# A three-layer kernel: the start of its first feed-forward layer as a written list

## The chip, the cores and the metric

The kernel runs on one NeuronCore of a Trainium2 chip. The engines are TensorE (PE in the rows; its weight loads PEld), VectorE (DVE), ScalarE (ACT), GpSimd (POOL) and SyncE (SP), which here only issues DMAs. Each runs its own queue of instructions in order and waits on semaphores for the others. The metric is the time of one execution on the device in microseconds; a comparison uses the median of several runs.

## The reference

Inputs q, k, v have shape (4, 8, 768, 64): batch, heads, tokens, features. Three layers follow each other:

```
# 1: linear attention with a decay gamma[h] per head
state = gamma * state + outer(k[t], v[t]);  y[t] = q[t] @ state / sqrt(64)      for t in 0..767
x = y as (3072 tokens, 512)
# 2: first feed-forward layer, 512 -> 2048 -> 512
h = x @ w_in;  x = (h * cos(h)) @ w_out
# 3: second feed-forward layer, 512 -> 1536 -> 512
g = x @ w_gate;  out = (silu(g) * (x @ w_val)) @ w_out2
```

## The kernel before

**Tiles.** The 3072 tokens are 24 chunks of 128: six blocks along the sequence for each of four batch rows. Chunks 4j to 4j+3 (one block of all four rows) form token tile j, 512 tokens wide. Chunks 0 to 3 need no state: scores (`scores_pe`), decay (`scores_decay`, three VectorE products for each half), values (`values_pe`). Chunks from 4 on use halves of a chunk: near scores (`near_pe`), a state update (`update_pe`, `update_add`), and values out of the old state and the near scores (`near_values`). GpSimd scales keys (`scale_keys`), queries (`scale_queries`) and the state. The values are split into a high and a low part for the matmuls: ScalarE writes the high one (`split_hi`), VectorE the low one (`split_lo`).

**Units.** The first feed-forward layer works in units. Unit n belongs to a token tile j and a slice m of 128 hidden features. Its hidden product is 12 matmuls of 512 columns (high by high, high by low, low by high, over four slices of features), from `project`. Then come: the turns n (ScalarE), the remainder r (VectorE), Sin and Square (ScalarE), the product with h (VectorE), the high half of g (ScalarE), the low half (VectorE). `output1` multiplies g into four output banks, 12 matmuls, two units later (`SKEW = 2`). Units 0 to 6 are tile 0 with slices 0 to 6 (`HEAD = 7`), unit 7 on is tile 1 from slice 0. After output unit 6 the four banks are evacuated, two by ScalarE and two by VectorE, and stored to DRAM (`x2d`) by four DMAs. Hidden products share two banks (`ps_h`), so the product of unit n waits until unit n-2 has read its own for the last time, in the VectorE product with h.

**Weights.** The 16 slices of weights of this layer come in 64-bit words, 1 MB for each slice, and are converted: abs (ScalarE), clamp (GpSimd), shift of the exponent (`low`, VectorE), `round` (ScalarE), `merge` (VectorE), `hi` (ScalarE), `lo` (VectorE). Weights 0 to 6 are loaded at the start and stay. Weights 7 to 10 and 12 to 15 are loaded later, into the tiles that chunks 7 to 4 and 3 to 0 held before.

**What sets the order.** The kernel writes the order of each engine by hand (`manual_schedule`): what the program calls first stands first on its engine. Before the units a short string lists the work on chunks 0 to 4 and weights 0 and 1. In each unit, `hidden1` places its own steps and those of the weights that `halves_at` gives it (first halves `a`, second halves `b`), and lists of late work (`late_g`, `late_gl`, `late_mid`, `late_x`) are run at fixed places in it. `attn_at` says after which unit the products of chunks 4 to 7 stand. SP issues the loads in the order of the calls. TensorE gets some matmuls with no use (`keep_awake`) in the stretch in which it waits for loads.

Of the kernel before, what the change touches and what calls it, by code (L numbers as in the profile page):

```python
# [46 lines left out]
HEAD = 7  # L47

# [48 lines left out]
def fused(ctx: ExitStack, tc: tile.TileContext, qkv, w1, w2, consts, out):  # L97
# [53 lines left out]
    class Weight:  # L151
# [89 lines left out]
    W1, W2 = [], []  # L241

    def fetch_w1(m):
        assert m == len(W1)
        W1.append(Weight(w1[m], wpool, f"w{m}", w1d.get(m)))
# [39 lines left out]

    qkv_t = {}
# [3 lines left out]
    def load_qk(c, pool=qpool, tag="qkv"):  # L290
        if c >= NCH:
            return
        if pool is wpool:
            both = wpool.tile([P, 4, 512], F32, tag=tag, name="qkv")
            qkv_t[c] = [both[:, 0:2], both[:, 2:4]]
        else:
            qkv_t.setdefault(c, [None, None])[0] = pool.tile([P, 2, 512], F32, tag=tag, name="qk")
        nc.sync.dma_start(out=qkv_t[c][0].rearrange("p a b -> p (a b)"), in_=qkv[c, :, 0:1024])

    def load_kv(c, part=slice(0, 2)):  # L300
        if c >= NCH:
            return
        if qkv_t.setdefault(c, [None, None])[1] is None:
            qkv_t[c][1] = qpool.tile([P, 2, 512], F32, tag="qkv", name="kv")
        n0, n1 = 512 * part.start, 512 * part.stop
        nc.sync.dma_start(
            out=qkv_t[c][1][:, part].rearrange("p a b -> p (a b)"), in_=qkv[c, :, 1024 + n0:1024 + n1]
        )
# [58 lines left out]
    def values_pe(c, places=((ps_a, "a"), (ps_a, "a")), idle=0):  # L367
# [3 lines left out]
        ps_t[c, "rest"] = y2[0][:, 2:4].rearrange("p a (b d) -> p (a b) d", d=D)  # L371
# [51 lines left out]
    def update_add(c, u):  # L423
        st = states[c % B]
        if u == 0:
            nc.vector.tensor_tensor(out=middle, in0=ps_t[c][0][:, 1], in1=st, op=ALU.add)
            return
        old_state[c] = st
        if last_block(c):
            return  # L430
        new = states[c % B] = spares.pop()
        nc.vector.tensor_tensor(out=new, in0=ps_t[c][1][:, 1], in1=middle, op=ALU.add)
        nc.gpsimd.tensor_tensor(
            out=new, in0=new, in1=const(CG, NP).unsqueeze(2).to_broadcast([P, NP, D]), op=ALU.mult
        )
# [5 lines left out]
    def near_values(c, places=((ps_a, "a"), (ps_a, "a"))):  # L441
        qk, kv = qkv_t[c]
        y2 = [p.tile([P, 4, C], F32, tag=t, name="y") for p, t in places]
        y = [t[:, 0:2] for t in y2]
        order = [h for pair in ((0, 2), (1, 3)) for k in pair for h in FEATURES[k]]
# [32 lines left out]
    def state_pe(c, place=(ps_a, "a")):  # L478
        _, kv = qkv_t[c]
        rest = ps_t.pop((c, "rest"))  # L480
        u = place[0].tile([P, NP, D], F32, tag=place[1], name="u") if place else rest
# [10 lines left out]
    def state_add(c):  # L492
        u, st = ps_t.pop((c, "u")), states[c % B]
        nc.vector.tensor_copy(out=st, in_=u)
# [3 lines left out]

    def attn_state(c, place):
        state_pe(c, place)  # L500
        late_mid.append(lambda: state_add(c))
# [6 lines left out]
    def attn_update(c):  # L508
        update_pe(c)
        late_mid.extend(lambda u=u: update_add(c, u) for u in range(2))  # L510
# [52 lines left out]
    def hidden1(j, m, first, a, b, soon):  # L563
        begin(first)
        if not soon:
            each(a, "size")
        h = project(weight1(m, 0), x_t[j], ps_h, "h", "h")
        n = npool.tile([P, T], I32, tag="n", name="n")
        r = tmp.tile([P, T], F32, tag="r", name="r_")
# [5 lines left out]
        nc.scalar.activation(out=n, in_=h, func=AF.Identity, scale=TURN)  # L575
        each(b, "hi")
        if soon:
            each(a, "size")
        each(a, "round")
        run(mid)  # L580
        nc.vector.scalar_tensor_tensor(
            out=r, in0=h, scalar=TURN, in1=n, op0=ALU.mult, op1=ALU.subtract
        )
# [3 lines left out]
        nc.scalar.activation(out=r, in_=r, func=AF.Sin, scale=PI)  # L587
        nc.scalar.activation(out=r, in_=r, func=AF.Square, scale=ROOT2)

        def finish():  # L590
            nc.vector.scalar_tensor_tensor(
                out=r, in0=r, scalar=1.0, in1=h, op0=ALU.subtract, op1=ALU.mult
            )
            g = g_t[1, j, m] = gpool.tile([P, 2, T], F32R, tag="g", name="g")
            nc.scalar.activation(out=g[:, 0], in_=r, func=AF.Copy, scale=-1.0)
            late_gl.append(lambda: nc.vector.scalar_tensor_tensor(
                out=g[:, 1], in0=r, scalar=-1.0, in1=g[:, 0].bitcast(F32), op0=ALU.mult, op1=ALU.subtract
            ))

        late_g.append(finish)  # L600
# [137 lines left out]
    ORDER = ["P1", "P2", "P5", "P6", "P3", "P7", "P4"]  # L738
    next_wo = [0]

    def fetch_wo():
        g, n = divmod(next_wo[0], len(ORDER))
        if g < len(groups2):
# [4 lines left out]
                in_=wod[groups2[g][1]][ORDER.index(order_of(g)[n])],  # L748
# [77 lines left out]
    def order_of(g):  # L826
        return ["P1", "P5", "P2", "P6", "P3", "P7", "P4"] if g == len(groups2) - 1 else ORDER
# [36 lines left out]
    def second_layer():  # L864
# [145 lines left out]
    o2, o3, two = (ps_o, "o2"), (ps_o, "o3"), [(ps_a, "a")] * 2  # L1010

    attn_at = {
        0: [(attn_state, c, place) for c, place in enumerate(two + [o2, o3])]
        + [(attn_update, 4), (scale_queries, 4), (scale_keys, 5)],
        1: [(attn_scores, 5), (attn_values, 4, (o2, o3), False), (attn_update, 5), (scale_keys, 6)],
        2: [(attn_values, 5, two, False)], 3: [(attn_near, 6), (scale_keys, 7)],
        4: [(attn_values, 6, two, False)],
        5: [(attn_near, 7)], 6: [(attn_values, 7, two, False)],
    }
# [43 lines left out]
    with tc.manual_schedule():  # L1063
        warm = tmp.tile([P, T], F32, tag="r", name="warm")
# [9 lines left out]
        queries = slice(CQ, CQ + 512)  # L1074
        head = slice(CG, CQ)
        near = slice(CD, CD + 512)
        keys, values = slice(0, 1), slice(1, 2)
        places = ["w15", "w14", "w13", "w12", "w10", "w9", "w8", "w7"]

        def load_cst(cols):  # L1080
            nc.sync.dma_start(out=const(cols.start, cols.stop - cols.start), in_=consts[:, cols])

        load_qk(0, wpool, places[0])
        for half in range(2):
            nc.sync.dma_start(out=first_dec[half], in_=consts[:, 512 * half:512 * half + 512])
        load_kv(0, values)
        nc.vector.memset(above, ABOVE)
        nc.scalar.activation(out=idle_act, in_=above, func=AF.Sin, scale=2.0**-16)
        load_qk(1, wpool, places[1])
        load_kv(1, values)  # L1090
        fetch_w1(0)
        for c in (2, 3):
            load_qk(c, wpool, places[c])
            load_kv(c, values)
        fetch_w1(1)
        load_cst(head)
        load_kv(0, keys)
        load_qk(CPB, wpool, places[CPB])
        load_cst(near)
        for c in range(1, CPB):  # L1100
            load_kv(c, keys)
        load_cst(queries)
        fetch_w1(2)
        load_kv(CPB)
        load_qk(CPB + 1, wpool, places[CPB + 1])
        load_kv(CPB + 1)
        fetch_w1(3)
        for c in (CPB + 2, CPB + 3):
            fetch_w1(len(W1))
            load_qk(c, wpool, places[c])  # L1110
            load_kv(c)
        fetch_w1(6)

        def first_scores(c):
            if c == CPB:
                near_pe(c, [(ps_o, f"o{half}") for half in range(2)])
                return
            scores_pe(c, [(ps_o, f"o{2 * (c % 2) + half}") for half in range(2)], 4 if c else 0)

        def first_decay(c):  # L1120
            for half in range(2):
                near_decay(c, half) if c == CPB else scores_decay(c, half, c % 2)

        def first_y(c):
            values_pe(c, [(ps_h, "h")] * 2 if c % 2 else [(ps_a, "a")] * 2, 10)

        def first_hi(c):
            first_x[c] = values_x(c)
            for y, x in first_x[c]:
                split_hi(y, x)  # L1130

        def first_lo(c):
            for y, x in first_x[c]:
                split_lo(y, x)

        first_x = {}
        steps = {
            "sc": first_scores, "m": first_decay, "y": first_y, "xh": first_hi,
            "xl": first_lo, "k": scale_keys,
        }  # L1140
        for a in (
            "sc0 m0 y0 sc1 xh0 xl0 m1 size0 y1 xh1 xl1 low0 round0 sc2 m2 y2 merge0 xh2 sc3 m3 hi0 xl2 lo0 size1 "
# [121 lines left out]
```

## Time and profile before

| | us |
|---|---|
| median of 3 runs | 1141.17 |
| lowest and highest | 1140.91, 1143.11 |
| the profiled execution | 1140.55 |
| its span, first to last instruction | 1138.4 |
| TensorE matmuls busy | 1120.1 (98% of the span) |
| VectorE busy | 795.4 (70%) |
| ScalarE busy | 627.0 (55%) |
| GpSimd busy | 120.2 (11%) |

The span is what the rows speak of; about 2 us lie around it. Busy shares are means over the whole execution. The changed part lies in its first 90 us, so windows and timelines of that part are to be read, not the means. Matmuls overlap, so the time of one is best read from the start of one piece to the start of the next.

### The profile page before, as it was taken

The numbers are of one execution on the slowest core, as the hardware profiler recorded it, in microseconds if no ns is written. First come the engines' busy times: TensorE is split into PE (matmuls) and PEld (weight loads), VectorE is DVE, ScalarE is ACT, GpSimd is POOL, SyncE is SP. The second block draws the span as 40 slices with busy tenths as digits, with TensorE's granted clock in tenths as the row PEclk, the third lists the DMA queues.
The fourth block names the chain that finished last, engine by engine and source line by source line (L and its number), as shares of the span: only waits on it lengthen the run. The fifth ranks groups of instructions, "written<-read, shape, count | busy, mean of one in ns | idle before, by whom it ended". The sixth has DMA issues, their size and how long they took to land.

```text
span 1138.4 us, 19049 instructions
## 1 busy us (share of the span) xinstructions
PE 1120.1 (98%) x7704; PEld 914.2 (80%) x7704; DVE 795.4 (70%) x1267; ACT 627.0 (55%) x954; POOL 120.2 (11%) x109
## 2 busy tenths in 40 slices
PE   8899999999999999999999999999999999999998
PEld 5688878888888888888888888887888887888886
DVE  6865774457777677667656566878666879666687
ACT  4868974456667767677755343434343434333431
POOL 3521222111211111110000000000000000000011
PEclk9899999999999999999999999999999999999999
DMA  9616843235997699588774845676656675655534
GB/s 349 244 39 235 318 173 107 86 137 190 330 355 275 246 358 387 192 316 341 277 272 165 318 173 202 256 260 215 237 207 228 230 282 209 230 214 203 185 139 166
DMA packets 62966, 266.00 MB, mean 234 GB/s; under 512 B 6304, under 2 KB 6560, under 8 KB 47264
## 3 DMA queue, kind: packets, MB, share of 16 engines
q1 hardware_dynamic: 62880, 264.80, 63.4%
q8 instruction: 60, 0.98, 0.4%
q14 instruction: 26, 0.21, 0.1%
HBM read 208.68 MB, written 56.10 MB: 233 GB/s over the span
## 4 chain that ended last, share of the span: by engine, by line
PE 83%; ACT 6%; DVE 5%; DMA 4%; issue 1%; SPq 0%; POOL 0%; DVEq 0%; POOLq 0%
PE h L532 20%; PE o L618 20%; PE X L757 15%; PE Z L757 8%; PE oX L843 7%; PE oZ L843 6%; PE Y L757 4%; ACT rw L176 2%; DMA qkv<-in_qkv_dram 2%; DMA kv<-in_qkv_dram 2%; PE y L452 1%; PE y L463 1%; ACT f L160 1%; DMA rw<-in_w_dram 1%; DVE go L804 1%; DVE acc L854 1%
## 5 line engine op out<-in xcount | busy, mean ns | idle before, releaser
L532 PE MATMUL h<-x,w 128*128 128x512 f32 x780 | 191.5, 394 | 2.1 <-DVE x L146 1.4
L618 PE MATMUL o<-g,w 128*128 128x512 f32 x780 | 189.0, 391 | 2.0 <-DVE x L146 2.0
L618 PEld LDWEIGHTS o<-g,w 128*128 128x128 f32 x780 | 147.0, 189 | 33.0 <-issue 2.4
L532 PEld LDWEIGHTS h<-x,w 128*128 128x128 f32 x780 | 144.2, 188 | 34.1 <-DVE x L146 1.6
L757 PE MATMUL X<-xo,wh 128*128 128x512 f32 x576 | 145.4, 389 | 0.0
L757 PEld LDWEIGHTS X<-xo,wh 128*128 128x128 f32 x576 | 108.0, 188 | 22.7 <-DVE xo L718 0.4
L843 PE MATMUL oX<-go,wo 128*128 128x512 f32 x432 | 109.1, 389 | 0.3 <-DVE acc L854 0.3
L804 DVE TENSOR_TENSOR go<-raw,go 128x512 fp32r<-128x512 f32 x126 | 84.6, 709 | 35.0 <-ACT go L802 34.7
L843 PEld LDWEIGHTS oX<-go,wo 128*128 128x128 f32 x432 | 81.0, 188 | 17.5 <-DVE acc L854 0.7
L575 ACT ACTIVATE n<-h 128x512 int32<-128x512 f32 x96 | 57.0, 594 | 66.5 <-PE h L532 65.8
L532 PE MATMUL h<-x,back 128*128 128x512 f32 x372 | 91.0, 393 | 0.0
L176 ACT ACTIVATE rw<-rw,above 128x1024 uint16<-128x1024 uint32 x34 | 89.4, 2629 | 0.0
L618 PE MATMUL o<-g,back 128*128 128x512 f32 x372 | 89.4, 389 | 0.0
L618 PEld LDWEIGHTS o<-g,back 128*128 128x128 f32 x372 | 69.8, 188 | 14.5
L532 PEld LDWEIGHTS h<-x,back 128*128 128x128 f32 x372 | 68.9, 188 | 14.9
L802 ACT ACTIVATE go<-raw 128x512 fp32r<-128x512 f32 x126 | 72.2, 622 | 15.6 <-DVE raw L795 9.9
L843 PE MATMUL oZ<-go,wo 128*128 128x512 f32 x312 | 78.8, 389 | 0.0
L757 PE MATMUL X<-x,wh 128*128 128x512 f32 x288 | 73.4, 390 | 2.8 <-DVE p L980 2.8
L757 PE MATMUL Z<-xo,wh 128*128 128x512 f32 x288 | 73.1, 389 | 0.0
L843 PEld LDWEIGHTS oZ<-go,wo 128*128 128x128 f32 x312 | 58.6, 188 | 12.2
L795 POOL TENSOR_TENSOR raw<-raw 128x512 f32<-128x512 f32 x7 | 10.1, 1450 | 551.2 <-DVE go L804 551.2
L757 PEld LDWEIGHTS X<-x,wh 128*128 128x128 f32 x288 | 53.8, 188 | 15.0 <-issue 2.8
(683 smaller groups left out, 1686.7 us busy)
## 6 DMA issues: line engine op xcount, KB each, us to landing
wh<-w2d SPq DMA_DIRECT2D x36, 1024.0 KB, 6.2
rw<-in_w_dram SPq DMA_DIRECT2D x34, 1024.0 KB, 7.7
wo<-wod SPq DMA_DIRECT2D x63, 512.0 KB, 3.7
back<-w1d SPq DMA_DIRECT2D x31, 1024.0 KB, 7.8
wh<-w2d SPq DMA_DIRECT2D x36, 768.0 KB, 4.8
w2d<-parts SPq DMA_DIRECT2D x12, 1024.0 KB, 4.1
xo<-x2d SPq DMA_DIRECT2D x19, 512.0 KB, 6.7
w1d<-w SPq DMA_DIRECT2D x9, 1024.0 KB, 4.8
```

Source lines behind the costliest of these rows:

```text
L160: nc.scalar.activation(out=self.f, in_=self.raw[:, :, 1].bitcast(F32), func=AF.Abs)
L176: nc.scalar.activation(out=self.raw.bitcast(U16)[:, :, 2], in_=self.raw[:, :, 0].bitcast(U32), func=AF.Identity, scale=2.0**-29, bias=above,)
L452: nc.tensor.matmul(out=y[bank][D * half:D * half + D, slot, HALF * u:HALF * u + HALF], lhsT=st[r, h // 2, :], rhs=qk[r, 0, q0:q0 + HALF], ...
L463: nc.tensor.matmul(out=y[bank][D * half + f:D * half + f + width, slot, HALF * u:HALF * u + HALF], lhsT=kv[r, 1, h * D + f:h * D + f + wid ...
L532: nc.tensor.matmul(out=ps, lhsT=w[:, a, k * P:(k + 1) * P], rhs=x[:, b, k, :], start=n == 0, stop=n == len(order) - 1,)
L575: nc.scalar.activation(out=n, in_=h, func=AF.Identity, scale=TURN)
L618: nc.tensor.matmul(out=o_t[0][i], lhsT=w[:, a, i * P:(i + 1) * P], rhs=g[:, b, :], start=first and n == 0, stop=last and n == 2,)
L757: nc.tensor.matmul(out=ps, lhsT=w[:, a, k * P:(k + 1) * P], rhs=x[:, b, k, :], start=start and n == 0, stop=n == len(order) - 1, skip_grou ...
L802: nc.scalar.activation(out=t[:, i, 0], in_=raw_of(g, i, slot), func=AF.Copy)
L804: nc.vector.tensor_tensor(out=t[:, i, 1], in0=raw_of(g, i, slot), in1=t[:, i, 0].bitcast(F32), op=ALU.subtract)
L843: nc.tensor.matmul(out=ps, lhsT=w[:, i, a, d * P:(d + 1) * P], rhs=x[:, i, b, :], start=start and m == 0, stop=m == len(order) - 1, skip_g ...
L854: nc.vector.tensor_tensor(out=e[:, c], in0=ps[:, c], in1=e[:, c], op=ALU.add)
```

## The change

The string of steps and the calls per unit up to unit 8 are replaced by three tables: `LOADS` (the order of the first loads), `ORDER` (every step on chunks 0 to 7, weights 0 to 6, hidden units 0 to 8 and output units 0 to 6), and `BANKS` (the banks of scores, state products and values). `AWAKE` gives the useless matmuls ahead of three steps: 39, before 52. The list was found by a search over a model of the engines. From unit 9 on the program is as before. `size` becomes `abs` and `clamp`, which the list places apart; keys and values of a chunk are loaded by one function, `load_first`; the state's copy and its decay are two steps; the class `Hidden` holds the steps of a unit. In the list a number is a chunk, a weight or a unit: `h`, `n`, `r`, `sin`, `sq`, `fin`, `ghi`, `glo` are the steps of a hidden unit in the order given above, `o` an output unit, `u` a state product, `U` an update, `y` values, `sc` scores, `da` and `db` the decay of a chunk's halves.

```diff
+SCRIPT = 9
+LOADS = """
+    qk0 dec qk1 w1 v0 qk2 w0 qk3 v1 v3 v2 k2 k0 head k1 w3 qk4 k4 w2 k3 near queries qk5 qk6 v4 k5 w4 v5 k7 v6
+    k6 w5 qk7 w6 v7
+""".split()
+ORDER = """
...
+    ghi5 xb7 sin6 sq6 Xb7 fin6 glo5 h7 h8 o5 n7 ghi6 r7 glo6 o6 n8 r8 sin8 sin7 sq8 sq7 fin7 ghi7 glo7
+""".split()
+AWAKE = {"sc1": 10, "y0": 14, "sc3": 15}
...
+        for name, c in map(split_name, ORDER):
+            if name in steps:
+                steps[name](c)
+            elif hasattr(Hidden, name):
+                getattr(hidden[c], name)()
+            else:
+                getattr(W1[c], name)()
+        late_g.append(hidden[SCRIPT - 1].late)
+        pending.extend(units[SCRIPT - 2:SCRIPT])
+        del w1_halves[:2 * HEAD]
+        fetch_w1(HEAD)
+
-        for n, (kind, j, m, first, last) in enumerate(units):
+        for n, (kind, j, m, first, last) in list(enumerate(units))[SCRIPT:]:
```

What moves, in the order of the instructions. First TensorE around the first hidden unit, before; `u` are state products, `sc` scores or (L409, after L442) updates, `h` hidden units, `w_403`, `w_461` the weights 0 and 1:

```order
L376 MATMUL y<-s,qkv 64x128 x8
L394 MATMUL sc<-qkv 64x64 x16
L532 MATMUL h<-x,w_403 128x512 x12
L484 MATMUL u<-qkv 64x64 x32
L409 MATMUL sc<-qkv 64x64 x16
L532 MATMUL h<-x,w_461 128x512 x12
```

The same place after (there `w_465` is weight 0 and `w_401` weight 1):

```order
L518 MATMUL u<-qkv 64x64 x16
L427 MATMUL sc<-qkv 64x64 x16
L518 MATMUL u<-qkv 64x64 x8
L565 MATMUL h<-x,w_465 128x512 x12
L518 MATMUL u<-qkv 64x64 x8
L565 MATMUL h<-x,w_401 128x512 x12
L442 MATMUL sc<-qkv 64x64 x16
L427 MATMUL sc<-qkv 64x64 x32
```

The state products of chunks 0 to 2 now stand ahead of hidden unit 0, that of chunk 3 between units 0 and 1.

ScalarE around the evacuation of output unit 6 (`ev`), before; `r__1118` belongs to unit 7, `r__1155` to unit 8, `rw_1139` is weight 7:

```order
L587 ACTIVATE r__1118<-r__1118 128x512
L588 ACTIVATE r__1118<-r__1118 128x512
L595 ACTIVATE g<-r__1118 128x512
L575 ACTIVATE n<-h 128x512
L587 ACTIVATE r__1155<-r__1155 128x512
L588 ACTIVATE r__1155<-r__1155 128x512
L545 ACTIVATE ev<-o_707 128x512
L545 ACTIVATE ev<-o_709 128x512
L160 ACTIVATE f<-rw_1139 128x1024
L595 ACTIVATE g<-r__1155 128x512
```

The same place after; `r__1138` belongs to unit 7, `r__1167` to unit 8, `rw_1177` is weight 7:

```order
L578 ACTIVATE ev<-o_841 128x512
L578 ACTIVATE ev<-o_843 128x512
L605 ACTIVATE n<-h 128x512
L614 ACTIVATE r__1167<-r__1167 128x512
L614 ACTIVATE r__1138<-r__1138 128x512
L617 ACTIVATE r__1167<-r__1167 128x512
L617 ACTIVATE r__1138<-r__1138 128x512
L626 ACTIVATE g<-r__1138 128x512
L185 ACTIVATE f<-rw_1177 128x1024
L626 ACTIVATE g<-r__1167 128x512
```

The evacuations now stand ahead of the turns of unit 8 and of the Sin and Square of both units.

SP's loads and stores at that place, before (`x2d` are the stores of the evacuated banks, `rw` loads of weights, `w1d` the write back of a converted weight):

```order
L155 DMA rw_1139<-in_w_dram 128x2048
L628 DMA x2d_90<-ev 128x512 x4
L155 DMA rw_1188<-in_w_dram 128x2048
L155 DMA rw_1234<-in_w_dram 128x2048
L195 DMA w1d_96<-w_1256 128x2048
```

And after:

```order
L687 DMA x2d_90<-ev 128x512 x4
L180 DMA rw_1177<-in_w_dram 128x2048
L180 DMA rw_1179<-in_w_dram 128x2048
L180 DMA rw_1225<-in_w_dram 128x2048
L226 DMA w1d_96<-w_1246 128x2048
```

The load of weight 7 stood ahead of the four stores and now stands behind them.

## Rows read from the trace of the kernel before

**Rows 1.** The page, part 4: the chain of waits, by engine.

```profile
PE 83%; ACT 6%; DVE 5%; DMA 4%; issue 1%; SPq 0%; POOL 0%; DVEq 0%; POOLq 0%
```

**Rows 2.** TensorE's timeline: start, length, line, operation, count, idle before and its releaser.

```profile
5.32 1.22 PE L345 MATMUL sc<-qkv 64*64 64x128 f32 x32 [0.27 <-DMA qkv<-in_qkv_dram]
...
27.60 2.08 PE L484 MATMUL u<-qkv 128*64 128x64 f32 x64
...
47.00 2.90 PE L618 MATMUL o<-g,w 128*128 128x512 f32 x6 [2.04 <-DVE x L146]
...
51.31 3.04 PE L532 MATMUL h<-x,w 128*128 128x512 f32 x12
...
57.00 0.69 PE L394 MATMUL sc<-qkv 64*64 64x64 f32 x32
57.52 0.65 PE L409 MATMUL sc<-qkv 64*64 64x64 f32 x32
58.09 3.02 PE L532 MATMUL h<-x,w 128*128 128x512 f32 x12
...
63.76 0.69 PE L452 MATMUL y<-qkv,st 64*64 64x64 f32 x32
...
65.00 3.02 PE L532 MATMUL h<-x,w 128*128 128x512 f32 x12
...
86.97 2.88 PE L618 MATMUL o<-g,w 128*128 128x512 f32 x12
89.69 2.88 PE L532 MATMUL h<-x,w 128*128 128x512 f32 x12
```

**Rows 3.** Waits of TensorE (90 to 200 us), ScalarE (90 to 160): total, times, longest.

```profile
PE h L532 <- DVE w L146: 0.3, 1, 0.3
PE h L532 <- DVE r__1566 L591: 0.3, 1, 0.3
...
ACT n L575 <- PE h L532: 1.3, 2, 1.0
```

**Rows 4.** ScalarE's timeline.

```profile
34.64 1.21 ACT L160 ACTIVATE f<-rw 128x1024 f32<-128x1024 f32 x1 [0.56 <-DMA rw<-in_w_dram]
...
87.17 0.60 ACT L575 ACTIVATE n<-h 128x512 int32<-128x512 f32 x1 [1.40 <-PE h L532]
...
89.20 0.63 ACT L588 ACTIVATE r__1155<-r__1155 128x512 f32<-128x512 f32 x1
89.73 1.07 ACT L545 ACTIVATE ev<-o 128x512 f32<-128x512 f32 x2
90.69 1.12 ACT L160 ACTIVATE f<-rw 128x1024 f32<-128x1024 f32 x1
...
103.49 0.60 ACT L575 ACTIVATE n<-h 128x512 int32<-128x512 f32 x1 [0.98 <-PE h L532]
```

**Rows 5.** GpSimd's timeline: four scalings of keys.

```profile
22.14 6.46 POOL L313 TENSOR_TENSOR qkv<-qkv,cst 128x512 f32<-128x512 f32 x4
```

**Rows 6.** VectorE's timeline.

```profile
41.30 1.78 DVE L168 TENSOR_SCALAR f<-f 128x1024 int32<-128x1024 int32 x1
...
49.43 0.69 DVE L168 TENSOR_SCALAR f<-f 128x1024 int32<-128x1024 int32 x1
...
89.90 0.69 DVE L547 COPY ev<-o 128x512 f32<-128x512 f32 x1 [0.20 <-PE o L618]
90.50 0.68 DVE L591 SCALAR_TENSOR_TENSOR r__1155<-r__1155,h 128x512 f32<-128x512 f32 x1
```

**Rows 7.** A window: us, TensorE busy (matmuls), granted clock, DMA share, GB/s.

```profile
47.00:48.00 1.00, 1.00 (x3) 0.50 0.00 0
```

**Rows 8.** SP's timeline, and the landing of the loads of line 155.

```profile
31.92 44.63 SPq L155 DMA_DIRECT2D rw<-in_w_dram  x2
...
93.33 0.92 SPq L155 DMA_DIRECT2D rw<-in_w_dram  x2
...
DMA to landing us min/median/max: 4.8/8.7/15.5
```

More of the change, by code (lines that the diff above doesn't have):

```diff
@@ L163, in size @@
             )
+        def size(self):
+            self.abs()
+            self.clamp()
         def low(self):
@@ L288, in fused, with load_qk, load_kv, load_first @@
     x_t = {}
-    def load_qk(c, pool=qpool, tag="qkv"):
+    def load_qk(c):
         if c >= NCH:
             return
[L293 to L297, printed above, removed]
+        qkv_t.setdefault(c, [None, None])[0] = qpool.tile([P, 2, 512], F32, tag="qkv", name="qk")
         nc.sync.dma_start(out=qkv_t[c][0].rearrange("p a b -> p (a b)"), in_=qkv[c, :, 0:1024])
-    def load_kv(c, part=slice(0, 2)):
+    def load_kv(c):
         if c >= NCH:
             return
[L303 to L308, printed above, removed]
+        qkv_t.setdefault(c, [None, None])[1] = qpool.tile([P, 2, 512], F32, tag="qkv", name="kv")
+        nc.sync.dma_start(out=qkv_t[c][1].rearrange("p a b -> p (a b)"), in_=qkv[c, :, 1024:2048])
+    def load_first(what, c):
+        if c not in qkv_t:
+            both = wpool.tile([P, 4, 512], F32, tag=FIRST_PLACES[c], name="qkv")
+            qkv_t[c] = [both[:, 0:2], both[:, 2:4]]
+        n0, n1, part, i = {"qk": (0, 1024, 0, slice(0, 2)), "k": (1024, 1536, 1, 0), "v": (1536, 2048, 1, 1)}[what]
+        dst = qkv_t[c][part][:, i]
+        if what == "qk":
+            dst = dst.rearrange("p a b -> p (a b)")
+        nc.sync.dma_start(out=dst, in_=qkv[c, :, n0:n1])
     def scale_keys(c):
@@ L432, in update_add, with near_values @@
         nc.vector.tensor_tensor(out=new, in0=ps_t[c][1][:, 1], in1=middle, op=ALU.add)
-        nc.gpsimd.tensor_tensor(
-            out=new, in0=new, in1=const(CG, NP).unsqueeze(2).to_broadcast([P, NP, D]), op=ALU.mult
-        )
     spares = [spare]
-    def near_values(c, places=((ps_a, "a"), (ps_a, "a"))):
+    def near_values(c, places=((ps_a, "a"), (ps_a, "a")), idle=0):
         qk, kv = qkv_t[c]
@@ L476, in values_x, with state_pe @@
         return [(y[n], x_t[j][:, :, 2 * n:2 * n + 2, o:o + C]) for n in range(2)]
-    def state_pe(c, place=(ps_a, "a")):
+    first_u = []
+    def state_pe(c, places):
         _, kv = qkv_t[c]
-        rest = ps_t.pop((c, "rest"))
-        u = place[0].tile([P, NP, D], F32, tag=place[1], name="u") if place else rest
+        if c % SESSION == 0:
+            first_u[:] = [p.tile([P, 2, NP, D], F32, tag=t, name="u") for p, t in places]
+        u = first_u[c % 2][:, c // 2 % 2]
         for h in range(H):
@@ L490, in state_pe, with state_copy, state_decay @@
         ps_t[c, "u"] = u
-    def state_add(c):
-        u, st = ps_t.pop((c, "u")), states[c % B]
-        nc.vector.tensor_copy(out=st, in_=u)
+    def state_copy(c):
+        nc.vector.tensor_copy(out=states[c % B], in_=ps_t.pop((c, "u")))
+    def state_decay(c):
+        st = states[c % B]
         nc.gpsimd.tensor_tensor(
@@ L509, in attn_update @@
         update_pe(c)
-        late_mid.extend(lambda u=u: update_add(c, u) for u in range(2))
+        late_mid.append(lambda: update_add(c, 0))
+        late_mid.append(lambda: (update_add(c, 1), None if last_block(c) else state_decay(c)))
     def attn_near(c):
@@ L561, in begin, with __init__, h, n @@
             run(late_x)
-    def hidden1(j, m, first, a, b, soon):
-        begin(first)
[L565 to L569, printed above, removed]
+    class Hidden:
+        def __init__(self, j, m):
+            self.j, self.m = j, m
+        def h(self):
+            self.ps = project(weight1(self.m, 0), x_t[self.j], ps_h, "h", "h")
+        def n(self):
+            self.turns = npool.tile([P, T], I32, tag="n", name="n")
+            nc.scalar.activation(out=self.turns, in_=self.ps, func=AF.Identity, scale=TURN)
+        def r(self):
+            self.t = tmp.tile([P, T], F32, tag="r", name="r_")
+            nc.vector.scalar_tensor_tensor(
+                out=self.t, in0=self.ps, scalar=TURN, in1=self.turns, op0=ALU.mult, op1=ALU.subtract
+            )
+        def sin(self):
+            nc.scalar.activation(out=self.t, in_=self.t, func=AF.Sin, scale=PI)
+        def sq(self):
+            nc.scalar.activation(out=self.t, in_=self.t, func=AF.Square, scale=ROOT2)
+        def fin(self):
+            nc.vector.scalar_tensor_tensor(
+                out=self.t, in0=self.t, scalar=1.0, in1=self.ps, op0=ALU.subtract, op1=ALU.mult
+            )
+        def ghi(self):
+            self.g = g_t[1, self.j, self.m] = gpool.tile([P, 2, T], F32R, tag="g", name="g")
+            nc.scalar.activation(out=self.g[:, 0], in_=self.t, func=AF.Copy, scale=-1.0)
+        def glo(self):
+            nc.vector.scalar_tensor_tensor(
+                out=self.g[:, 1], in0=self.t, scalar=-1.0, in1=self.g[:, 0].bitcast(F32),
+                op0=ALU.mult, op1=ALU.subtract,
+            )
+        def late(self):
+            self.fin()
+            self.ghi()
+            late_gl.append(self.glo)
+    def hidden1(j, m, first, a, b):
+        begin(first)
+        each(a, "size")
+        u = Hidden(j, m)
+        u.h()
         run(late_g)
@@ L586, in hidden1 @@
         each(a, "low")
[L587 to L600, printed above, removed]
+        u.sin()
+        u.sq()
+        late_g.append(u.late)
     part = []
@@ L1007, in fused @@
     n6 = len(units)
[L1010 to L1019, printed above, removed]
+    attn_at = {}
     for i in range(CPB):
@@ L1073, in fused @@
             nc.tensor.matmul(out=idle, lhsT=wz[:, :P], rhs=wz[:, :T], start=True, stop=True)
[L1074 to L1085, printed above, removed]
@@ L1086, in fused @@
-        load_kv(0, values)
         nc.vector.memset(above, ABOVE)
         nc.scalar.activation(out=idle_act, in_=above, func=AF.Sin, scale=2.0**-16)
[L1089 to L1136, printed above, removed]
@@ L1150, in fused, with split_name @@
-        late_mid.append(lambda: first_decay(CPB))
-        del w1_halves[:4]
+        parts = {"head": slice(CG, CQ), "near": slice(CD, CD + 512), "queries": slice(CQ, CQ + 512)}
+        def split_name(a):
+            name = a.rstrip("0123456789")
+            return name, int(a[len(name):] or 0)
+        for name, c in map(split_name, LOADS):
+            if name == "dec":
+                for half in range(2):
+                    nc.sync.dma_start(out=first_dec[half], in_=consts[:, 512 * half:512 * half + 512])
+            elif name in parts:
+                cols = parts[name]
+                nc.sync.dma_start(out=const(cols.start, cols.stop - cols.start), in_=consts[:, cols])
+            elif name == "w":
+                fetch_w1(c)
+            else:
+                load_first(name, c)
```

94 lines of the change are left out of this document (57 added, 37 removed).

## Prediction

> **What bounds the kernel now.** I read the chain of waits first. 83% of the span on it is TensorE [rows 1], so a change counts only where it lets TensorE finish the same matmuls earlier. The changed part is the start, so the second view was TensorE's timeline from 0 to 130 us [rows 2]. The last output matmul of the first group (output unit 6) begins at 86.97 us and the next hidden unit (unit 9) at 89.69 us; from 51.31 us on no row of that timeline has idle time before it. The third view was the waits of TensorE from 90 to 200 us: 0.3 us twice [rows 3]. From 89.69 us to the end the two programs hold the same TensorE work in the same order, so a shift of TensorE there goes through to the end, if ScalarE, which converts the weights, shifts with it. ScalarE was the fourth view: between 90 and 160 us it waits for a hidden product twice, 1.3 us in all [rows 3], the last time at 103.49 us, 0.98 us, for that of unit 11 [rows 4]. So two numbers decide: when output unit 6 ends (before: 89.69), and how long after that the product of unit 11 ends (before: five pieces of 2.72 us later, 103.3).
>
> **The list up to output unit 6.** Pieces of TensorE, from start to start [rows 2]: a hidden or output unit 2.72 us (86.97 to 89.69); near scores of a chunk 0.52 (57.00 to 57.52); a state update 0.57 (57.52 to 58.09); near values 1.24 (63.76 to 65.00); the four state products 2.08 together.
>
> When the first state product starts depends on loads. By the rows, 0.52 MB had landed at 5.32 us (the first scores waited for it) and 11.53 MB at 34.6 us, when ScalarE waited for weight 3 [rows 2, 4]: 0.376 MB per us. In the new list of loads 6.55 MB are asked for up to the keys of chunk 1, so these land at about 21.4 us. GpSimd scales chunk 1 and then chunk 0, 1.62 us each (four took 6.46 [rows 5]), so the state products start at 24.7. Before, they started at 27.60, but after the first hidden unit; now that unit stands behind three of them and the scores of chunk 4.
>
> From 24.7 on TensorE has 9 hidden and 7 output units (16 x 2.72 = 43.5 us), 2.1 of state products, 4 x 0.52 of scores, 4 x 0.57 of updates and 4 x 1.24 of near values: 54.9 us, and the end would be 79.6 us without a wait. I see two waits in the order. The fourth state product stands ahead of hidden unit 1 and needs the keys of chunk 3: 9.70 MB, landed at 29.7, scaled at 31.3, while TensorE is through at 24.7 + 1.6 + 0.5 + 2.7 = 29.5: 1.8 us. The update of chunk 5 stands ahead of hidden unit 2 and needs the values of chunk 5: 13.1 MB, 38.8 us, while TensorE comes there at 31.3 + 0.5 + 2.7 + 0.6 + 1.0 + 1.2 = 37.3: 1.5 us. Output unit 6 then ends at 82.9. The repeated warm-up matmuls, the bank changes and the split of the abs from the clamp are inside this sum: all of them lie before 24.7 us or beside a load or key that is waited for. Without that cover the 39 warm-up matmuls would be TensorE time. Bounds: 79.6 if both waits are hidden, 87 if VectorE cannot keep up (a rival, below). I take 82.9; the gain up to here is 89.7 - 82.9 = 6.8 us.
>
> **What the end of the list gives back.** The list puts output unit 6 with its four evacuations ahead of the turns of unit 8 on ScalarE, and the sine of 8 ahead of that of 7. Call the end of output unit 6 T. Hidden unit 9 has only two banks to choose from, and takes that of unit 7, which comes free with the last VectorE product of unit 7. Before, that product lay ahead of the evacuations. Now the chain is: ScalarE's second evacuation ends at T + 0.1 (VectorE's last one started 0.21 us after TensorE's end, 89.90 against 89.69 [rows 6, 2], ScalarE's is one group of matmuls, 0.68, earlier, and takes 0.5 [rows 4]); turns, remainder, sine and square of a unit need 2.03 us to the square's start (87.17 to 89.20 [rows 4]); the sine of 7 and the square of 8 stand in between, about 0.5 each; the square takes 0.63, VectorE's product 0.69 [rows 6]. T + 0.1 + 2.03 + 1.0 + 0.63 + 0.69 = T + 4.5. TensorE stands idle for 4.5 us, with everything behind hidden unit 9 queued.
>
> That idle time has a second price. After 2.04 us idle, TensorE started at 47.00 with a granted clock of 0.50, the lower level of 1.2 GHz [rows 2, 7], and needed 4.31 us (47.00 to 51.31) for half an output unit and near values, 1.36 + 1.24 at the higher level: 1.7 us lost. After a longer idle time I expect the same fall. Bounds 0 and 3.4 (twice); I take 1.7.
>
> The load of weight 7 is the third place. SP issued it ahead of the four stores before, and had it out by 76.5 us [rows 8]; now it stands behind them in SP's queue, so it goes out at T + 1.3 (last evacuation T + 0.9; two issues took 0.92 at 93.33), with the loads of weights 8 and 9, and the write back of 7, queued behind it. A weight took 4.8 us at least from issue to landing and 8.7 at the median [rows 8]. ScalarE needs it for the abs of unit 9, and behind that abs the high half of unit 8, the turns of unit 9 and the rest wait. From that abs to the wait for unit 11 ScalarE had 12.8 us before (90.69 to 103.49 [rows 4]), about 1.8 of it idle. Landed at T + 6.1 to T + 7, ScalarE is ready for unit 11 at T + 17.1 to 18; TensorE has that product at T + 4.5 + 1.7 + 5 x 2.72 = T + 19.8. So it is hidden, and costs nothing; without that cover, at the median of 8.7 (landing at T + 10), it would cost 1.2 us.
>
> **Sum.** Gain 6.8, given back 4.5 + 1.7: 0.6 us, rounded up to 0.8 because some of the early idle time before may vanish as well. Against the profiled execution that is 1138.4 - 0.8 = 1137.6 of span and 1139.7 with the 2.15 us around it (1140.55 - 1138.4); this execution lies 0.6 under the median of 1141.17, so the forecast is **1140.4 us**.
>
> **A rule that speaks against the change.** VectorE's shift of a weight's exponent took 1.78 us at 41.30, with GpSimd at work, and 0.69 at 49.43, with GpSimd idle [rows 6]. The Trainium skill (SBUF — State Buffer, Who interferes with whom) states that VectorE and GpSimd hold their shared port pair for a whole instruction and the other one fully blocks; these two rows agree with it.
>
> **The rivals.**
> - *The stage wins more than the tail takes.* The clock stays up over the idle 4.5 us, or the waits for keys are shorter: gain 79.6 to 81.5 for T, so 8.2 to 10.1, less 4.5 to 6.2: 2 to 5.6 us, time 1135.6 to 1139, middle 1137.3. For it: nothing but the loads stands against it up to 40 us, and those were the slowest part of the estimate. Against it: the row at 47.00.
> - *VectorE becomes the bound (the slower side).* Between the first hidden unit (27 us) and hidden unit 4 (about 53), the list packs on VectorE the exponent shifts, merges and low halves of four weights beside the scalings of eight keys and queries on GpSimd. One shift that meets a GpSimd instruction loses 1.1 us [rows 6]. I count ten weight instructions there; if nine of them lose 1.1 us beyond what the walk holds, hidden unit 4 and so T is late by 9.9, less the 3 or so that VectorE has to spare: T at about 89.7, nothing won, the tail still paid: 1141.2 + 6.2 = 1147.4 at worst. It decides from T = 86 on (two thirds of that), 1143.7. For it: the pair of rows. Against: GpSimd's work is no more than before.
> - *Weight 7 lands late* (T + 10 or later): ScalarE decides after T, 1.2 us or more: 1141.6 to 1143.
> - *The tail doesn't stall*, because the product of unit 7 is not behind the evacuations: gain 6.8, 1134.4. The order of ScalarE and VectorE speaks against it.
>
> **Chances.** The forecast 0.47 (own range 1138.7 to 1142.5); the stage wins more 0.27; no stall 0.05; VectorE bound 0.14; weight 7 late 0.07. A measurement of this kernel tells about 0.2%, 2.3 us, from no change (the three runs of before span 2.2). Faster than 1138.9: the two winning cases, nearly whole, 0.31. Slower than 1143.5: the VectorE case, part of the late weight, a little of the forecast: 0.18. Within: 0.51. The range goes from 1136.2, the lower part of the first rival, to 1144.0, the point from which VectorE decides.
>
> **What the changed profile would show.** State products from about 24.7 us; waits of TensorE for GpSimd or a load ahead of the fourth one and of the update of chunk 5; output unit 6 ending near 83 us; then TensorE idle 4.5 us, released by VectorE's product of unit 7, and a granted clock of 0.50 behind it; ScalarE waiting for weight 7. I am wrong if unit 9 starts within 1 us of output unit 6's end, if output unit 6 ends after 86 us, or if ScalarE reaches unit 11 after TensorE.

## The result: 0.7% slower, and the profile after

The changed kernel takes 1150.25 us (median of 4 runs, 1149.26 to 1151.12), the one before 1141.62 in the same series (4 runs, 1140.91 to 1143.11): 1.0074 times, 95% interval 1.0056 to 1.0091. The forecast was 1140.4, its range ended at 1144.0. The profiled execution took 1149.69 us with a span of 1147.9, at a mean granted clock of 0.994 (before: 1138.4 at 0.997).

TensorE's share of the chain of waits fell from 83% [rows 1] to 81%:

```profile
PE 81%; DVE 6%; ACT 6%; DMA 5%; POOL 1%; issue 1%; SPq 0%; DVEq 0%; POOLq 0%
```

TensorE's timeline after, in the columns of [rows 2]:

```profile
25.39 1.64 PE L518 MATMUL u<-qkv 128*64 128x64 f32 x32 [3.39 <-POOL qkv L346]
26.96 1.13 PE L427 MATMUL sc<-qkv 64*64 64x64 f32 x32
28.02 1.12 PE L518 MATMUL u<-qkv 128*64 128x64 f32 x16
29.07 3.06 PE L565 MATMUL h<-x,w 128*128 128x512 f32 x12
32.06 0.69 PE L518 MATMUL u<-qkv 128*64 128x64 f32 x16
...
35.62 0.69 PE L442 MATMUL sc<-qkv 64*64 64x64 f32 x32
...
41.04 1.20 PE L483 MATMUL y<-qkv,st 64*64 64x64 f32 x31 [3.08 <-DVE st L465]
...
43.23 1.13 PE L442 MATMUL sc<-qkv 64*64 64x64 f32 x32
44.29 3.96 PE L565 MATMUL h<-x,w 128*128 128x512 f32 x12
48.18 0.69 PE L483 MATMUL y<-qkv,st 64*64 64x64 f32 x32
...
68.84 3.01 PE L565 MATMUL h<-x,w 128*128 128x512 f32 x12 [1.55 <-DVE r__880 L620]
...
86.88 5.60 PE L677 MATMUL o<-g,w 128*128 128x512 f32 x24
96.80 4.60 PE L565 MATMUL h<-x,w 128*128 128x512 f32 x12 [4.32 <-DVE r__1138 L620]
101.24 2.91 PE L677 MATMUL o<-g,w 128*128 128x512 f32 x12
...
109.42 2.88 PE L565 MATMUL h<-x,w 128*128 128x512 f32 x12
112.14 2.20 PE L677 MATMUL o<-g,w 128*128 128x512 f32 x9
...
164.56 0.69 PE L427 MATMUL sc<-qk 64*64 64x64 f32 x32
```

The row of the kernel before that the last one is to be held against, the scores of chunk 8:

```profile
155.68 0.69 PE L394 MATMUL sc<-qk 64*64 64x64 f32 x32
```

The bottom rows first. Output unit 6 ends where the idle time before hidden unit 9 begins, 96.80 - 4.32 = 92.48: 2.8 us later than the 89.69 of before, where 6.8 us earlier was forecast. Then come the idle time and a hidden unit of 4.44 us (96.80 to 101.24) in place of 2.72. The scores of chunk 8 start 8.9 us later than before (164.56 against 155.68). These 8.9 us go through to the end (span + 9.5), as the prediction's first part had it. So the price of the tail of the list is as forecast, and the question is the 9.6 us by which output unit 6 is late against the 82.9 forecast.

VectorE's timeline after shows where its first part comes from:

```profile
36.37 0.42 DVE L452 TENSOR_TENSOR s<-sc,cst 128x256 f32<-128x256 f32 x1 [4.18 <-PE sc L442]
...
39.20 0.41 DVE L452 TENSOR_TENSOR s<-sc,cst 128x256 f32<-128x256 f32 x1
...
40.57 0.42 DVE L465 TENSOR_TENSOR st<-sc,st 128x256 f32<-128x256 f32 x1
...
67.34 0.76 DVE L452 TENSOR_TENSOR s<-sc,cst 128x256 f32<-128x256 f32 x2 [4.16 <-PE sc L442]
68.01 0.68 DVE L620 SCALAR_TENSOR_TENSOR r__880<-r__880,h 128x512 f32<-128x512 f32 x1
```

Line 452 is the decay of a chunk's near scores (da and db), line 442 its state update (U). The scores of chunk 4 were there by 28.0. But the list calls U4 two hidden units after these scores and still ahead of da4, and both use the two banks of chunk 4 (the scores lie in one half of each tile, the update writes the other). So da4 waits for U4, VectorE stands idle 4.18 us with its queue behind it: a state copy, two steps of the conversion of weight 2, and only then the second decay (db4, 39.20) and the state. So the state for chunk 4's values (line 465) comes so late that TensorE idles 3.08 us until 41.04. Chunk 7 repeats it: 4.16 us of VectorE, 1.55 us of TensorE ahead of 68.84.

The granted clock, in the window view (us, busy time and count of TensorE, its weight loads, VectorE, ScalarE, GpSimd, then the clock, DMA share, GB/s):

```profile
25.00:27.00 2.00, 1.61 (x36) 1.50 (x36) 2.00 (x6) 2.00 (x3) 2.00 (x3) 0.71 1.00 402
27.00:29.00 2.00, 2.00 (x50) 1.84 (x48) 2.00 (x2) 1.49 (x1) 2.00 (x2) 0.50 1.00 378
...
41.00:43.00 2.00, 1.96 (x80) 1.85 (x80) 2.00 (x3) 1.72 (x3) 2.00 (x2) 0.50 1.05 422
...
98.00:101.00 3.00, 3.00 (x8) 2.30 (x8) 0.73 (x2) 1.68 (x2) 1.04 (x1) 0.51 1.00 415
```

It is at 0.50, the 1.2 GHz level, behind each of the three long idle times. The forecast had counted that for the last alone.

ScalarE's two rows on weight 7: its wait for the load, and its wait for the product of unit 11:

```profile
98.55 1.16 ACT L185 ACTIVATE f<-rw 128x1024 f32<-128x1024 f32 x1 [1.14 <-DMA rw<-in_w_dram]
...
112.34 0.60 ACT L605 ACTIVATE n<-h 128x512 int32<-128x512 f32 x1 [1.03 <-PE h L565]
```

### The profile page after: what moved, and what is told of

Same layout as the page of the kernel before. It is cut to its first block, busy times and chain, and to the rows that moved or that the text cites. A ratio compares the mean times of both kernels' runs of the same rounds, so it can differ in the third digit from the quotient of the medians.

```text
span 1147.9 us, 19034 instructions
## 1 busy us (share of the span) xinstructions
PE 1120.4 (98%) x7691; PEld 915.1 (80%) x7691; DVE 793.7 (69%) x1267; ACT 626.1 (55%) x954; POOL 122.4 (11%) x109
## 4 chain that ended last, share of the span: by engine, by line
PE 81%; DVE 6%; ACT 6%; DMA 5%; POOL 1%; issue 1%; SPq 0%; DVEq 0%; POOLq 0%
PE h L565 19%; PE o L677 19%; PE X L816 15%; PE Z L816 8%; PE oX L902 7%; PE oZ L902 6%; PE Y L816 4%; DMA qkv<-in_qkv_dram 2%; DMA kv<-in_qkv_dram 2%; ACT rw L207 2%; PE y L483 1%; DVE go L863 1%; PE y L494 1%; DVE acc L913 1%; ACT f L185 1%
## 5 line engine op out<-in xcount | busy, mean ns | idle before, releaser
L565 PE MATMUL h<-x,w 128*128 128x512 f32 x780 | 194.1, 398 | 6.6 <-DVE r__1138 L620 4.3
L902 PEld LDWEIGHTS oZ<-go,wo 128*128 128x128 f32 x312 | 58.6, 188 | 12.2
```

The lines of the kernel that those rows point to most:

```text
L565: nc.tensor.matmul(out=ps, lhsT=w[:, a, k * P:(k + 1) * P], rhs=x[:, b, k, :], start=n == 0, stop=n == len(order) - 1,)
L902: nc.tensor.matmul(out=ps, lhsT=w[:, i, a, d * P:(d + 1) * P], rhs=x[:, i, b, :], start=start and m == 0, stop=m == len(order) - 1, skip_g ...
```

## The experiments

Theory A: the loss up to output unit 6 comes from the two decays that wait for updates called before them, and from the low clock behind the idle time; the loss behind it is the tail. Rival B, the prediction's: VectorE is the bound, through GpSimd's port; then moving two decays gives nothing. Rival C: the idle times only pass on waits for loads and keys, which come back when they are removed.

Behind each measured time stand its ratio to the kernel before, measured in the same series, and the 95% interval of that ratio. The changed kernel's ratio was 1.0074. The medians of the kernel before were 1140.55 to 1141.62 us in the four series, so a difference in us to the changed kernel's 1150.25 is good to about 1 us.

**Tail: unit 7's product ahead of the evacuations.**

```diff
-    ... n7 ghi6 r7 glo6 o6 n8 r8 sin8 sin7 sq8 sq7 fin7 ghi7 glo7
+    ... n7 ghi6 r7 glo6 sin7 sq7 fin7 ghi7 n8 glo7 r8 sin8 sq8 o6
```

> The changed kernel with the end of the list put in another order: Sin, Square, product and high half of unit 7, and all steps of unit 8 up to its Square, ahead of output unit 6 and its evacuations. Theory A (the end of the list costs 4.3 us of idle TensorE and 1.7 us of half clock): hidden unit 9 starts with output unit 6's end, no clock of 0.50 there; but weight 7 still goes out behind the stores and lands about 6.2 us after output unit 6, so ScalarE reaches unit 11 some 17 us after it instead of 13.6, and of the 6.0 us about 2.4 come back: 1147.8 us. Rival (the idle time is only where a lag of VectorE shows): the wait moves to the next hidden unit, 1150.

Measured 1150.18 (1.0081, 1.0065 to 1.0096): nothing gained, where 2.4 us were expected. Hidden unit 9 follows at once (92.22), but ScalarE's timeline shows the load of weight 7, hidden until now, as the next thing late:

```profile
91.74 0.60 ACT L578 ACTIVATE ev<-o 128x512 f32<-128x512 f32 x1 [0.30 <-PE o L677]
100.34 1.12 ACT L185 ACTIVATE f<-rw 128x1024 f32<-128x1024 f32 x1 [8.01 <-DMA rw<-in_w_dram]
101.36 0.62 ACT L626 ACTIVATE g<-r__1149 128x512 fp32r<-128x512 f32 x1
```

The high half of unit 8 stands behind it, so output unit 8 waits, and the clock falls in its turn:

```profile
102.04 0.73 PE L677 MATMUL o<-g,w 128*128 128x512 f32 x2 [1.49 <-ACT g L626]
103.85 4.15 PE L677 MATMUL o<-g,w 128*128 128x512 f32 x10 [1.08 <-DVE g L629]
```

**Weight 7 alone: its load called right behind the values of chunk 7, ahead of the stores.**

```diff
-        for name, c in map(split_name, ORDER):
+        for a, (name, c) in zip(ORDER, map(split_name, ORDER)):
             if name in steps:
                 steps[name](c)
+                if a == "y7":
+                    fetch_w1(HEAD)
...
         del w1_halves[:2 * HEAD]
-        fetch_w1(HEAD)
```

> The changed kernel with the load of weight 7 issued right behind the values of chunk 7 instead of behind the stores of output unit 6; nothing else. Theory A: ScalarE no longer waits for weight 7 (1.1 us before), but TensorE's late unit 9 and 11 cover that: 1150.2, no change within 0.5 us. Rival (the late load is what costs): 3 us or more come back, 1147 or less.

Measured 1152.21 (1.0096, 1.0081 to 1.0112). The wait of 4.32 us is unchanged, as expected; the load was hidden behind it. The 2 us more are not explained by the tail: output unit 6 ended 1.2 us later in its trace, because hidden unit 0, in part still at the lower clock, took 3.66 us for 3.06, and the state product behind it then waited 0.40 us for keys. How long it stays low there differs from run to run (the last section); whether the earlier load adds to it stays open.

**Both.** The two edits above.

> Both edits of the two runs before: the end of the list in the other order and the load of weight 7 early. Theory A: nothing waits behind output unit 6, all 6.0 us come back: 1144.2. If the load had no share, it would give what the end of the list alone gives.

Measured 1144.89 (1.0035, 1.0024 to 1.0047), 5.4 us less than the changed kernel (4.5 by the ratios). The rows are without a wait:

```profile
87.90 5.60 PE L677 MATMUL o<-g,w 128*128 128x512 f32 x24
93.34 2.88 PE L565 MATMUL h<-x,w 128*128 128x512 f32 x12
...
104.22 2.88 PE L565 MATMUL h<-x,w 128*128 128x512 f32 x12
106.94 2.88 PE L677 MATMUL o<-g,w 128*128 128x512 f32 x12
```

The product of unit 11 ends 13.6 us behind output unit 6, as before the change. So the price of the tail, 4.3 + 1.7, is one of two losses in series: each edit alone gains nothing.

**The two decays ahead of the updates of their chunks** (tail unchanged).

```diff
-    h0 u3 h1 U4 abs2 ... merge3 st2 da4 st3 ... sc6 sc5 hi3 low2 merge2 db4 r0 ... sc7 o2 U7 hi5 da7 db7 fin3
+    h0 u3 h1 abs2 ... merge3 st2 da4 db4 st3 ... sc6 U4 sc5 hi3 low2 merge2 r0 ... sc7 da7 db7 o2 U7 hi5 fin3
```

> The changed kernel with the two decays of chunk 4 and of chunk 7 placed in the list ahead of the state update of that chunk, whose matmuls write the same two banks; the update of chunk 4 moves behind the scores of chunk 6. Theory A (VectorE stands 4.2 us twice because a decay waits for an update that was called before it): these two idle stretches go, values of chunk 4 start 3 us earlier, hidden unit 5 doesn't wait, and the fall of the clock at 39 us may go too: output unit 6 ends at 85 to 88 us instead of 92.5, time 1143 to 1146. Rival (VectorE is slowed by GpSimd at their shared port and is late anyway): VectorE's stall turns into work that is late, output unit 6 ends after 91, time 1149 or more.

Measured 1146.46 (1.0048, 1.003 to 1.0065): 3.8 us less (3.0 by the ratios, whose intervals just overlap; the slowest of its 4 runs, 1148.16, is faster than the fastest of the changed kernel's, 1149.26). Output unit 6 ends at 87.26, 5.2 us earlier. VectorE's decays have no wait, TensorE's wait ahead of chunk 4's values is 0.62, the clock stays at 1.00 there:

```profile
32.33 0.74 DVE L452 TENSOR_TENSOR s<-sc,cst 128x256 f32<-128x256 f32 x2
...
37.54 0.42 DVE L459 TENSOR_TENSOR st<-sc,st 128x256 f32<-128x256 f32 x1 [1.33 <-PE sc L427]
```

```profile
38.11 1.06 PE L483 MATMUL y<-qkv,st 64*64 64x64 f32 x30 [0.62 <-DVE st L459]
...
91.58 5.49 PE L565 MATMUL h<-x,w 128*128 128x512 f32 x12 [4.32 <-DVE r__1138 L620]
96.87 3.29 PE L677 MATMUL o<-g,w 128*128 128x512 f32 x12
```

VectorE does the same work beside the same work of GpSimd: B falls. For chunk 4 the edit does two things. It calls both decays ahead of the update, and it puts the second one ahead of the state copy and the two weight steps on VectorE, which took 2.5 us between the two decays in the changed kernel. No run moved only one of them, so how the 3 us ahead of chunk 4's values divide between the two is not shown. For chunk 7 VectorE's own order is unchanged.

The last two rows of TensorE show why 5.2 us became 3.8: behind the same 4.32 us the clock now stays low through hidden unit 9 and into output unit 7 (8.4 us for both, 7.2 in the changed kernel).

**The two decays one by one.** Chunk 4's part of that diff, and chunk 7's.

> The changed kernel with only the decays of chunk 4 called ahead of that chunk's state update. If both idle times of VectorE (4.18 us at 36.4, 4.16 us at 67.3) cost TensorE by themselves, this gains the wait of 3.08 us ahead of chunk 4's values less the 0.62 that stay, and the 2.6 us of low clock behind it, less the 1.55 us that belong to chunk 7 and stay: output unit 6 ends at about 88.7, the time is 1146.7. Rival: the wait ahead of chunk 4's values only passes on what GpSimd's scalings of queries and keys would make late anyway; then 1149 or more.

> The changed kernel with only the decays of chunk 7 called ahead of that chunk's state update. The wait of 1.55 us ahead of hidden unit 5 goes, everything before 60 us stays as it is: output unit 6 ends at about 90.9, the time is 1148.7. Rival: the next product of ScalarE or VectorE is as late, and the time stays at 1150.2.

Chunk 4: 1146.93 (1.0064, 1.0051 to 1.0077), output unit 6 ends at 88.32. The trace and the median are as expected, but the 5 runs reach from 1146.61 to 1150.55 and the interval overlaps that of the changed kernel, so the time alone does not show the gain. Chunk 7: 1150.3 (1.0084, 1.007 to 1.0098); not the 1.5 us expected. Its wait is gone from the trace, and between the values of chunk 4 and hidden unit 5 it is 1.1 us shorter, but this run's first state product came 0.6 us later and its clock stayed low longer. So chunk 4 is the larger part (4.2 of the 5.2 us at output unit 6, by the traces); chunk 7 is worth between nothing and 1.5 us.

**All three edits: tail, weight 7, both decays.**

> The changed kernel with three edits: the product of unit 7 ahead of the evacuations of output unit 6, the load of weight 7 issued ahead of the stores, and the two decays ahead of the state updates of their chunks. If the two losses are independent, it is 1146.5 less the 5.3 that the first two edits gained together without the third: 1141.2; and if the clock, which stayed low longer in the run with the decays alone (hidden units 9 and 10 took 5.49 and about 3.3), is held as well, about 1139. Output unit 6 ends at 87 to 88, hidden unit 9 follows without idle time, unit 11's product ends 13.6 us behind output unit 6. Rival: ScalarE has no slack left when TensorE is 5 us earlier (it then waits for weight 7 or converts weights late), and the time stays at 1143 or more.

Measured **1138.45** (11 runs, 1137.48 to 1139.72; before 1140.78, 27 runs): 0.998, 0.9971 to 0.9989. It beats both kernels.

```profile
25.47 1.98 PE L518 MATMUL u<-qkv 128*64 128x64 f32 x32 [3.38 <-POOL qkv L346]
...
29.49 4.01 PE L565 MATMUL h<-x,w 128*128 128x512 f32 x12
...
82.38 5.60 PE L677 MATMUL o<-g,w 128*128 128x512 f32 x24
87.82 2.88 PE L565 MATMUL h<-x,w 128*128 128x512 f32 x12
...
98.70 2.88 PE L565 MATMUL h<-x,w 128*128 128x512 f32 x12
101.42 2.88 PE L677 MATMUL o<-g,w 128*128 128x512 f32 x12
```

Output unit 6 ends 1.9 us ahead of the kernel before, unit 11 follows in 13.6: the new order does win, once nothing takes it back. The edits gain 11.8 us together and 5.4 + 3.8 = 9.2 apart (10.7 and 4.5 + 3.0 by the ratios); 1.2 of the rest is the low clock behind the tail's wait, longer in the run with the decays alone. Held against the run with tail and weight 7, the two decays are worth 6.4 us, and the runs of the two kernels do not overlap (at most 1139.72 against at least 1143.98).

**TensorE kept busy over the wait for keys.** All three edits, and:

```diff
             first_u[:] = [p.tile([P, 2, NP, D], F32, tag=t, name="u") for p, t in places]
+            if c == 0:
+                keep_awake(first_u[0][:, 0].rearrange("p a b -> p (a b)"), 27)
```

> As the kernel with all three edits, and 27 repeated 128x256 matmuls without use in the 3.4 us in which TensorE waits for the keys ahead of the first state product. If the idle time itself brings the granted clock down behind it, the first state products and the scores behind take their 2.1 us again instead of 3.7, hidden unit 0 starts 1.5 us earlier and output unit 6 ends 1.5 us earlier; the time is 1.5 us below that of the kernel with the three edits. Rival: GpSimd's keys of chunk 3 and 2 or the loads set the pace from the state products to chunk 4's values, and the 1.5 us come back as a wait there: no difference. Start of the first state product: 25.4 to 26 in both.

Measured 1139.31 (0.9991, 0.9983 to 1.0): no gain. The clock does stay up (1.00 from 25 to 29 us), hidden unit 0 starts 1.6 us earlier than with the three edits, and takes 1.0 us less. But the gain comes back:

```profile
27.86 3.01 PE L567 MATMUL h<-x,w 128*128 128x512 f32 x12
31.52 0.69 PE L520 MATMUL u<-qkv 128*64 128x64 f32 x16 [0.65 <-POOL qkv L346]
...
37.78 0.69 PE L483 MATMUL y<-qkv,st 64*64 64x64 f32 x32 [0.40 <-POOL qkv L354]
...
39.80 0.69 PE L442 MATMUL sc<-qkv 64*64 64x64 f32 x32 [0.70 <-POOL qkv L346]
40.42 1.20 PE L567 MATMUL h<-x,w 128*128 128x512 f32 x4
43.34 2.11 PE L567 MATMUL h<-x,w 128*128 128x512 f32 x8 [1.72 <-issue]
```

TensorE waits 1.75 us for GpSimd's keys and queries, and 1.72 us within hidden unit 2, a gap that the profile puts down to no engine; output unit 6 ends at 87.79, as with the three edits (87.82). For this stretch C is right in part: behind the low clock lie the keys, the wait that the prediction had expected. The cause of the 1.72 us stays open.

**Keys 0 and 1 loaded earlier.** All three edits, and:

```diff
-    qk0 dec qk1 w1 v0 qk2 w0 qk3 v1 v3 v2 k2 k0 head k1 w3 ...
+    qk0 dec qk1 w1 v0 qk2 w0 qk3 v1 v3 k0 head k1 v2 k2 w3 ...
```

> As the kernel with all three edits, but keys 0, the constants of the key scale and keys 1 are loaded ahead of values 2 and keys 2 (0.52 MB moved). GpSimd's first key scaling starts at about 20.7 instead of 22.1, the values of chunk 2 wait about 1 us longer, the idle time ahead of the first state product shrinks from 3.4 to about 1 us and its start moves from 25.4 to about 24. Gain 1.4 us, and up to 1.5 more if the clock then doesn't fall behind it: 0 to 3 us below the kernel with the three edits. Rival: the loads behind (values 2, keys 2) make the first hidden unit late, no difference.

Measured 1139.55 (0.9985, 0.9976 to 0.9995; 1136.59 to 1141.23): no difference from the three edits that these runs can tell. In its profile the wait for the keys is gone, the values of chunk 2 wait 2.10 us for a load in its place, and the clock is low there (0.66 from 20 to 25 us) and at 1.00 from 25 us on. That profile is of the fastest of the 11 runs, 3 us below their median, so its rows do not stand for all of them.

**The clock at the tail by itself.** The changed kernel, with matmuls without use between output unit 6 and hidden unit 9:

```diff
+        busy = ps_a.tile([P, T], F32, tag="a", name="busy")
+        for _ in range(18):
+            nc.tensor.matmul(
+                out=busy, lhsT=weight1(0, 0)[:, 0, :P], rhs=x_t[0][:, 0, 0, :], start=True, stop=True,
+                skip_group_check=True,
+            )
```

> The changed kernel with 18 repeated 128x512 matmuls without use (into a bank nothing else holds) between output unit 6 and hidden unit 9, where TensorE waits 4.3 us for VectorE's product of unit 7. The wait itself stays. If the lower clock behind it (hidden unit 9 at 4.44 us for 2.72) is due to the idle time, hidden unit 9 takes 2.7 to 3.0, and the time is 1.7 us less: 1148.5. Rival: the clock falls there whatever TensorE does, and the time stays at 1150.2.

```profile
92.95 4.24 PE L1203 MATMUL busy<-x,w 128*128 128x512 f32 x18
97.45 3.04 PE L565 MATMUL h<-x,w 128*128 128x512 f32 x12 [0.25 <-DVE r__1138 L620]
100.32 2.88 PE L677 MATMUL o<-g,w 128*128 128x512 f32 x12
```

With TensorE kept busy, hidden unit 9 takes 2.87 us where it took 4.44, so the idle time is what brings the clock down there, and 1.6 us its price in the trace. The time, 1149.72 (1.0079, 1.0066 to 1.0093), is 0.5 less than the changed kernel's, and its ratio is not below the 1.0074: the end-to-end runs neither show nor exclude the 1.7.

**Without the 39 warm-up matmuls.**

```diff
-AWAKE = {"sc1": 10, "y0": 14, "sc3": 15}
+AWAKE = {}
```

> The changed kernel without its 39 repeated 128x256 matmuls before 20 us. If they lie wholly beside waits and the loads and keys set the start of the first state product, that start stays at 25.4 and the time at 1150.2, whatever the clock does before 20 us. Rival: without them TensorE is idle for 1 to 2.5 us at a time, the values of chunks 0 to 3 run at the lower clock (4.3 us instead of the 4.2 they took in all where the clock was 1.0 would become up to 6 to 8) and the first state product starts up to 2 us later: 1152.

Measured 1150.15 (1.0078, 1.0066 to 1.0091), the same. The clock was 0.50 from 11 to 20 us, and the first state product still started at 24.77, behind a wait of 2.20 us for the keys. The profiled execution, 1148.27, is one of its faster ones (1148.06 to 1150.93). The cost of the matmuls is hidden, as forecast, and so is their use, as far as these runs tell.

## Why the prediction was wrong

- *What bounds the kernel*, that a shift at output unit 6 goes through to the end: right, 8.9 us at chunk 8's scores, 9.5 of span.
- *First state product at 24.7*: 25.39, released by GpSimd's key scaling, as the step said.
- **"I see two waits in the order"** is the step that failed. The list was read for what it needs from the loads and from GpSimd, and VectorE was taken to have 3 us to spare. The two waits named (the fourth state product, 1.8 us; the update of chunk 5, 1.5 us) did not occur in the changed kernel; output unit 6 ended after 86 us, one of the prediction's own signs of being wrong. The one that decided was not on the list: the decay of chunk 4 behind the update of chunk 4, 3.08 us of TensorE, and 1.55 for chunk 7. Moving these calls made output unit 6 end 5.2 us earlier.
- *The low clock* was counted at the tail alone. It also fell behind the wait for keys, where the state products and scores took 3.68 us (25.39 to 29.07), and behind the wait for chunk 4, where values, update of chunk 5 and hidden unit 2 took 7.14 (41.04 to 48.18). At a clock of 1.00 the same pieces took 2.41 us (25.45 to 27.86, TensorE kept busy) and 5.45 (39.26 to 44.71, all edits). That is 1.3 and 1.7 us for the clock.
- *2.72 us a unit*: too short a size for this stretch. That is the distance inside a run of hidden and output units; from a hidden unit to near scores or values it is about 2.95 (41.77 to 44.71 in the run with all edits). In the run with keys 0 and 1 earlier, at a clock of 1.00 from 25 us on, TensorE needed 61.2 us from the first state product to the end of output unit 6 (24.75 to 85.97), 2.6 of them waiting: 58.6 of work, 3.7 more than the 54.9 of the sum.
- The balance against 82.9: late start 0.7, clock 3.0, longer pieces 3.7, waits 5.0 (the two for decays, 4.6, and one of 0.39 for a state copy), less 3.3 for the two waits that did not come: 9.1 of 9.6 us. The rest was not split further.
- *The tail, 4.5 + 1.7*: 4.32 + 1.72, by the chain named. *Weight 7 hidden*: right. The product of unit 11 ended 19.7 us behind output unit 6 (forecast 19.8), and ScalarE, after 1.1 us of waiting for weight 7, still waited 1.03 for TensorE at unit 11. The first experiment shows what it costs when that cover is gone: all that the tail's edit wins.
- *VectorE the bound*, the rival on the slower side: the sign came, the mechanism did not. VectorE was idle for 4.2 us twice, the first time (32.2 to 36.4) in the very stretch in which it was to be short of time. The pair of rows behind it does repeat: the exponent shift took 1.53 us at 28.34, with GpSimd at work, and 0.68 at 37.04, begun while GpSimd stood idle. That agrees with the Trainium skill (SBUF — State Buffer, Who interferes with whom), and does not decide here.

## What to carry to other kernels

When an order is written out by hand, walk it for every engine, the idle-looking ones too, and ask of each instruction which earlier calls touch its tile or bank: an update that is called first and written late holds a reader that needs only the older half. An early gain must be followed to the next buffer and the next load: here two losses lay one behind the other, and removing either alone gave nothing. Price each long idle time of TensorE (here 3.08 to 4.32 us, and 2.04 before the change) with the clock that comes after it.

## What the runs showed of the hardware

- The same idle time costs unequally much behind it. After 4.32 us hidden unit 9 took 4.44 us in the changed kernel and 5.29 in the one with the decays moved (with 3.13 instead of 2.74 for the next unit), from start to start; after 3.4 us idle ahead of the state products, hidden unit 0 took 3.0 to 4.05 us in nine profiles with the same pieces ahead of it. Nor does the length of the idle time alone tell: after 2.04 us the clock was 0.50 in the kernel before [rows 2, 7], after 2.20 us in the run without warm-up matmuls it was 1.00 (25 to 29 us). How much of the spread between unprofiled runs lies there is not shown.
- 39 warm-up matmuls kept the clock at 1.00 from 11 to 20 us (0.50 without them) and moved nothing, since loads and keys set the pace there.
- The load of weight 7, issued at 93.7 us behind four stores and with two more loads behind it, was there 4.8 us later in the changed kernel (ScalarE's row at 98.55) and 6.7 us later in the first experiment (100.34), with the same queue. The forecast had taken 4.8 to 8.7.
